# Reordering the first weight loads, thinning the idle matmuls and dropping implied waits in a sliding-window attention and expert-layer kernel

## The chip, the cores and the metric

One core of one Trainium2 chip runs the whole program. The metric is device microseconds (us) per execution; lower is better. In the text S is one moment: the start of the first matmul of the second expert projection. The views name the engines PE (TensorE), DVE (VectorE), ACT (ScalarE), POOL (GpSimd) and SP (SyncE). A load or a transpose by DMA lands when its last part has arrived, and its time runs from issue to landing. TensorE's array has a slow state at the start: in the kernel before, the starts of matmuls of 128 columns are 107 ns apart until about 5.05 us, and 55 to 56 ns after it.

## The reference

Attention over 8 batches, 8 heads, 576 positions and head size 64, where each query sees only keys at most 32 positions away; then an expert layer on 4,608 tokens: 512 to 2,048, squared ReLU, back to 512.

```python
scores = scale * np.matmul(q, k.transpose(0, 1, 3, 2))
mask = np.abs(pos[:, None] - pos[None, :]) <= 32
scores = np.where(mask, scores, -1000000000.0)
attn = softmax(scores)                          # max, exp, sum, divide
x = np.matmul(attn, v).transpose(0, 2, 1, 3).reshape(4608, 512)
h = x @ w_in                                    # first projection
r = np.maximum(h, 0.0)
out = (r * r) @ w_out                           # second projection
```

## The kernel before

The kernel does not state its instruction order. It records operations with their reads and writes, and a list scheduler with assumed durations searches for one order for each engine; then it fills pauses of TensorE with idle matmuls and adds the semaphore waits. So every constant below can move instructions far away from the place where it seems to act.

```python
WARM, COLD, DENSE, SPARSE, EXTRA = 36000, 6000, 1.15, 0.95, 6     # idle matmuls
SIZES = (3,) * 9 + (4,) * 9                # chunks of a score group, after batch 0
ORDER = ("k01 q01 v00 v01 v02 k03 q03 v03 k04 q04 w10 v04 w11 w12 w13 k05 q05 ..."   # start of the loads
# ... (cut)
    def fill(self, out):
        at = 1200
        for op in sorted((o for o in out if o.eng == "PE"), key=lambda o: o.start):
            gap = min(op.start, WARM, self.first.start) - at
            one = 107 if at < COLD else 54
            for k in range(int((gap - 60) * (DENSE if at < COLD else SPARSE) // one) + (EXTRA if op is self.first else 0)):
                # ... (cut: one idle matmul of 128 columns on zeros)
# ... (cut), in emit: a wait is left out only if this engine already waited for as much of this semaphore
            for s, v in need.items():
                if waited.get((op.eng, s), 0) >= v:
                    continue
                waited[(op.eng, s)] = v
                e.wait_ge(sems[s] if s in sems else dsems[s], v)
# ... (cut), in vd_half: odd V products need V shifted by 64 rows, copied on VectorE
            self.p.rec("DVE", lambda e, d=dst, c=src: e.tensor_copy(d, c), reads=rd,
                       writes=[("vd", b % 2, s, lo) for s in range(s0, s1)], key=key, dur=80 + 145 * (s1 - s0), att=True)
# ... (cut), in xturn3: x of a trip of three chunks, transposed by DMA; plan is an allowance in ns
                self.p.rec("SP", lambda e, w=w, np=np, t0=t0: e.dma_start(
                    self.XT[:, :, t0:t0 + np], self.XR[0:np, 2 * y + w, :], transpose=True), ...)
                self.p.ops[-1].plan = 1500
```

In the names of the loads, w10 to w13 are the quarters of the first projection's weights; v03 and v04 are the V pieces that this text calls four and five, and k04 is the one that the texts call the fourth K piece. A chunk is 64 queries of one batch, nine to a batch. An odd chunk goes from its V piece through the copy `vd`, the product (line 778 before, 794 after), the division `xr` on VectorE, and a transpose on TensorE (807 before, 823 after) to `xt`, which the first projection reads (826 before, 842 after). The expert layer works in tiles of 512 tokens; tile 0 does 16 first-projection groups of 16 matmuls of 128 columns. "The third group" below is the third of these.

The softmax here doesn't subtract the row's maximum and nothing guards it: scores larger than these inputs give would overflow.

## Time and profile before

| what | before | how to read it |
|---|---|---|
| device time, first measurement | 300.18 us (299.93 to 300.94) | median of 3 runs |
| span of the profiled execution | 298.4 us | some 1.8 us of the device time lie outside it |
| TensorE busy | 98% | the bound; the rest is in the prediction |
| first group, fourth group | 18.21, 22.13 us | starts, in the order of time |
| S | 35.75 us | TensorE is full from here on |
| waits of TensorE after S | 0.43 us | one, ahead of tile 3 |
| idle matmuls | 103 of 128 columns | they compute nothing |

The kernel before in the order of time on TensorE (start, duration, engine, line, operation, output and inputs, tile, count), from the second group to S. After 22.13 no pause of any length is left:

```profile
19.57 1.06 PE L826 MATMUL ht<-xt,w 128*128 128x128 bf16 x16
...
20.73 1.05 PE L826 MATMUL ht<-xt,w 128*128 128x128 bf16 x16
21.89 0.40 PE L807 MATMUL outp<-identw,xr 128*128 128x128 bf16 x4
22.13 2.06 PE L826 MATMUL ht<-xt,w 128*128 128x128 bf16 x34
...
35.75 1.89 PE L919 MATMUL outp<-w,gt 128*128 128x512 bf16 x8
```

### The profile page before, as it was taken

To read this page: it belongs to the slowest core of one execution; us is meant where nothing else is said; L and a number is where in the kernel's file an instruction comes from. 1 tells how busy PE (TensorE), PEld (TensorE's weight loads), DVE (VectorE), ACT (ScalarE), POOL (GpSimd) and SP (SyncE) were. 2 spreads that over 40 slices of the span, in tenths; PEclk is the share of its full clock that TensorE was granted. 3 is DMA by queue.
4 is the path that set the end of the run, shared out by engine and by line. 5 is a ranking of instruction groups with operands and counts; after the bars stand their busy time and mean duration, and the time that the engine had idled before them with its cause. 6 is when DMAs were issued, how large, how long until landed. Compare 5 with 4: busy or idle time off the path is not lost.

```text
span 298.4 us, 7058 instructions
## 1 busy us (share of the span) xinstructions
PE 293.1 (98%) x2789; PEld 172.0 (58%) x2789; DVE 175.7 (59%) x428; ACT 160.5 (54%) x261; POOL 105.2 (35%) x131
## 2 busy tenths in 40 slices
PE   7899999999999999999999999999999999999996
PEld 7799855867668754544444545544445544444445
DVE  5864755674979966866386666773827682322200
ACT  3466543656657654763555656636645565444411
POOL 8999841332425434351254353313520000000000
PEclk9999999999999999999999999999999999999999
DMA  9999999999999999999499999999992230000022
GB/s 153 166 202 170 206 174 194 174 162 165 187 176 131 133 156 149 159 131 187 63 138 153 173 139 171 117 140 148 126 174 81 64 82 9 35 35 35 36 88 90
DMA packets 166817, 39.34 MB, mean 132 GB/s; under 512 B 157824, under 2 KB 162304, under 8 KB 166784
## 3 DMA queue, kind: packets, MB, share of 16 engines
q0 software_dynamic: 113120, 17.90, 89.8%
q1 hardware_dynamic: 46512, 11.15, 25.2%
q10 hardware_dynamic: 7152, 9.83, 10.1%
q8 instruction: 22, 0.36, 0.5%
q14 instruction: 11, 0.09, 0.1%
HBM read 36.70 MB, written 9.44 MB: 155 GB/s over the span
## 4 chain that ended last, share of the span: by engine, by line
PE 95%; DMA 2%; DVE 2%; issue 0%; POOL 0%; POOLq 0%
PE outp L919 41%; PE ht L867 28%; PE ht L849 7%; PE ht L826 7%; PE sc L703 3%; PE sc L647 3%; DMA qraw<-in_q_dram 2%; PE sc L495 1%; DVE vd L547 1%; PE outp L416 1%; PE sc L895 1%; PE outp L895 1%; DVE xr L791 1%; PE ht L495 0%; PE sc L751 0%; PE outp L807 0%
## 5 line engine op out<-in xcount | busy, mean ns | idle before, releaser
L919 PE MATMUL outp<-w,gt 128*128 128x512 bf16 x560 | 134.5, 379 | 0.0
L882 DVE TENSOR_TENSOR gt<-rt 128x512 bf16<-128x512 bf16 x144 | 59.5, 420 | 62.2 <-ACT rt L873 53.6
L867 PE MATMUL ht<-xt,w 128*128 128x512 bf16 x384 | 93.7, 379 | 0.3 <-issue 0.3
L919 PEld LDWEIGHTS outp<-w,gt 128*128 128x128 bf16 x560 | 52.9, 98 | 58.9
L873 ACT ACTIVATE rt<-ht 128x512 bf16<-128x512 f32 x96 | 57.4, 598 | 51.4 <-PE ht L867 48.9
L867 PEld LDWEIGHTS ht<-xt,w 128*128 128x128 bf16 x384 | 36.3, 98 | 41.9 <-issue 0.4
L469 POOL DMA_DIRECT2D qraw<-in_q_dram x39 | 33.6, 863 | 57.4 <-PE ht L867 20.6
L469 POOL DMA_DIRECT2D kraw<-in_k_dram x39 | 33.6, 860 | 35.1 <-PE ht L867 17.2
L535 POOL DMA_DIRECT2D vx<-in_v_dram x40 | 34.6, 866 | 21.3 <-PE ht L867 13.3
L684 DVE TENSOR_TENSOR pt<-e,mask 128x512 bf16<-128x512 bf16 (+1 forms) x63 | 29.9, 508 | 19.9 <-ACT e L668 19.1
L926 ACT ACTIVATE oe<-outp 128x512 f32<-128x512 f32 x35 | 20.9, 597 | 35.0 <-PE outp L919 34.9
L668 ACT ACTIVATE e<-sc 128x1024 bf16<-128x1024 f32 (+1 forms) x36 | 31.8, 917 | 6.4 <-PE sc L647 6.3
L727 DVE TENSOR_TENSOR xr<-pf,rs 128x512 bf16<-128x512 f32 (+1 forms) x42 | 27.5, 682 | 0.4
L826 PE MATMUL ht<-xt,w 128*128 128x128 bf16 x384 | 23.8, 219 | 0.0
L849 PE MATMUL ht<-xt,w 128*128 128x256 bf16 x192 | 23.3, 273 | 0.0
L826 PEld LDWEIGHTS ht<-xt,w 128*128 128x128 bf16 x384 | 21.7, 98 | 0.3
L720 DVE COPY pf<-sc 128x520 f32<-128x520 f32 x21 | 14.6, 697 | 8.8 <-PE sc L703 8.6
L849 PEld LDWEIGHTS ht<-xt,w 128*128 128x128 bf16 x192 | 18.0, 98 | 3.1
L717 ACT ACTIVATE pf<-sc 128x520 f32<-128x520 f32 x21 | 12.6, 602 | 13.0 <-PE sc L703 11.4
L834 ACT ACTIVATE rt<-ht 128x512 bf16<-128x512 f32 x24 | 14.2, 599 | 9.1 <-PE ht L826 8.8
L855 ACT ACTIVATE rt<-ht 128x512 bf16<-128x512 f32 x24 | 14.3, 600 | 6.0 <-PE ht L849 4.3
L722 DVE TENSOR_TENSOR pf<-pf 64x520 f32<-64x520 f32 x21 | 14.6, 697 | 2.2 <-ACT pf L717 1.2
(83 smaller groups left out, 180.3 us busy)
## 6 DMA issues: line engine op xcount, KB each, us to landing
out_dram<-oe ACTq DMA_DIRECT2D x35, 256.0 KB, 2.9
kraw<-in_k_dram POOLq DMA_DIRECT2D x30, 128.0 KB, 5.7
qraw<-in_q_dram POOLq DMA_DIRECT2D x30, 128.0 KB, 5.9
vx<-in_v_dram POOLq DMA_DIRECT2D x24, 128.0 KB, 5.4
w<-in_moe_w_in_dram POOLq DMA_DIRECT2D x4, 512.0 KB, 10.2
w<-in_moe_w_out_dram POOLq DMA_DIRECT2D x4, 512.0 KB, 16.4
vx<-in_v_dram POOLq DMA_DIRECT2D x16, 96.0 KB, 5.3
xt<-xr SPq DMA_TRANSPOSE x36, 4.0
```

The lines of the kernel that those rows point to most:

```text
L469: self.p.rec("POOL", lambda e: e.dma_start(dst, src), writes=[("fraw", b, t, x)], old=[("fraw", b - 2, t, y + (b == 2))], reads=self.pace( ...
L535: self.p.rec("POOL", lambda e: e.dma_start(self.VX[b % 2][r:r + n, s, :, 0:64], self.v[b, :, t0:t0 + n, :].rearrange("h p d -> p h d")), w ...
L668: self.p.rec("ACT", lambda e, d=dst, a=src: e.activation(d, a, ACTF.Exp, scale=0.125), reads=["s" + x for x in ("AC", "BD")[h]], writes=[( ...
L684: self.p.rec("DVE", lambda e: e.tensor_tensor(pt, ee, mb, ALU.mult), reads=[("e", g // 2)] + rd, writes=[("ptt", k)], old=old, key=key + k ...
L727: self.p.rec("DVE", lambda e, w=w, np=np: e.tensor_tensor(bass.AP(self.XR, 512 * (2 * y + w), [[2048, np], [64, 2], [128, 4], [1, 64]]), b ...
L826: mm = e.matmul(ht[:, 128 * (d % 4):128 * (d % 4) + 128], self.W1[:, ft, 128 * d:128 * d + 128], self.XT[:, ft, t0:t0 + 128], start=(ft == ...
L849: mm = e.matmul(ht[:, 256 * (d % 2):256 * (d % 2) + 256], self.W1[:, ft, 128 * d:128 * d + 128], self.XT[:, ft, 64 * s0:64 * s0 + 256], st ...
L867: mm = e.matmul(ht[:], self.W1[:, ft, 128 * d:128 * d + 128], self.XT[:, ft, 512 * T:512 * T + 512], start=(ft == 0), stop=(ft == 3))
L873: self.p.rec("ACT", lambda e: e.activation(rt[:], ht[:], ACTF.Relu), reads=[("ht", k % 2)], writes=[("rt", k % 4)], key=key, dur=560)
L882: self.p.rec("DVE", lambda e: e.tensor_tensor(g, r, r, ALU.mult), reads=[("rt", k % 4)], writes=tags, key=key, dur=430)
L919: mm = e.matmul(op, gt[:, d, 128 * u:128 * u + 128], self.W2[:, d, :], start=(d == 0), stop=(d == 15))
L926: self.p.rec("ACT", lambda e: e.activation(oe[:], op, ACTF.Copy), reads=[tag], writes=[("oe", x % 4)], key=key, dur=560)
```

## The change

Its intent: begin the expert layer sooner (the first weight quarter ahead of two V pieces), do not let idle matmuls delay real ones, take a load of copying off VectorE at the start, do more small score groups early and large ones late, and leave out waits that another wait already implies. Its core:

```diff
-WARM, COLD, DENSE, SPARSE, EXTRA = 36000, 6000, 1.15, 0.95, 6
+FIRST, WARM, COLD, DENSE, SPARSE, LASTF = 4000, 36000, 6000, 1.15, 0.7, 0.4
-SIZES = (3,) * 9 + (4,) * 9
+SIZES = (3,) * 13 + (4,) * 6
+VDACT = ((0, 0), (2, 0))
-ORDER = ("k01 q01 v00 v01 v02 k03 q03 v03 k04 q04 w10 v04 w11 w12 w13 ...
+ORDER = ("k01 q01 v00 v01 v02 k03 q03 k04 q04 w10 v03 w11 v04 w12 w13 ...
@@ fill @@
-        at = 1200
+        at = FIRST
@@ (cut: idle matmuls of 192 to 512 columns, fewer ahead of the first group) @@
@@ emit @@
-            for s, v in need.items():
-                if waited.get((op.eng, s), 0) >= v:
+            seen = known[op.eng]
+            while need:
+                s = max(need, key=...)              # the one that implies most of the others first
+                v = need.pop(s)
+                if seen.get(s, 0) >= v:
                     continue
-                waited[(op.eng, s)] = v
                 e.wait_ge(sems[s] if s in sems else dsems[s], v)
+                for x, y in at[(s, v)].items():     # what was known where that count was reached
+                    seen[x] = max(seen.get(x, 0), y)
@@ vd_half @@
+            if not b and (s0, lo) in VDACT:
+                self.p.rec("ACT", lambda e, d=dst, c=src: e.activation(d, c, ACTF.Copy), ...)
@@ load_w1 @@
-                   ... move=(32, 82 if d else 95, 500))
+                   ... move=(32, 82, 500 if d > 1 else 1300))
@@ (cut: memsets at the start merged) @@
```

In the built kernels the idle matmuls go from 103 with 13,184 columns to 15 with 6,848, the score groups after batch 0 from 18 to 19, and the waits over all engines from 1,525 to 1,169.

More of the change, by code (lines that the diff above doesn't have):

```diff
@@ L35 @@
 DEPTH, POST, BACK = 4000, {"POOL": 1500, "SP": 1000, "ACT": 1000}, {"POOL": 2500, "SP": 4000, "ACT": 4000}
-ORDER = ("k01 q01 v00 v01 v02 k03 q03 v03 k04 q04 w10 v04 w11 w12 w13 k05 q05 k10 q10 v10 k11 q11 v11 "
+ORDER = ("k01 q01 v00 v01 v02 k03 q03 k04 q04 w10 v03 w11 v04 w12 w13 k05 q05 k10 q10 v10 k11 q11 v11 "
          "w20 w21 w22 w23 k12 q12 v12 k13 q13 v13 k14 q14 v14").split()
@@ L315, in fill @@
             one = 107 if at < COLD else 54
-            for k in range(int((gap - 60) * (DENSE if at < COLD else SPARSE) // one) + (EXTRA if op is self.first else 0)):
+            cols = max(0, int((gap - 60) * (DENSE if at < COLD else LASTF if op is self.first else SPARSE) / one * 4)) * 32
+            t = at
+            while cols >= 192:
                 w = Op()
-                w.eng, w.fn, w.dma, w.deps, w.i = "PE", self.idle, None, {self.idle_on}, op.i
-                w.inc, w.val, w.sem, w.start, w.end, w.dur, w.key = False, None, None, min(at + one * k, op.start - 1), 0, one, -99
+                n = min(cols, 512)
+                w.eng, w.fn, w.dma, w.deps, w.i = "PE", (lambda e, n=n: self.idle(e, n)), None, {self.idle_on}, op.i
+                w.inc, w.val, w.sem, w.start, w.end, w.dur, w.key = False, None, None, min(t, op.start - 1), 0, one * n // 128, -99
                 out.append(w)
+                t, cols = t + w.dur, cols - n
             at = max(at, op.start + op.dur)
@@ L336, in emit @@
                 total[op.dma] = dcount[op.dma[0]] = dcount.get(op.dma[0], 0) + 16
-        waited = {}
+        known = {e: {} for e in engs}
+        at = {}
         for op in self.ops:
@@ L344, in emit @@
                 need[d.sem] = max(need.get(d.sem, 0), d.val)
-            for s, v in need.items():
-                if waited.get((op.eng, s), 0) >= v:
+            seen = known[op.eng]
+            while need:
+                s = max(need, key=lambda s: (s in sems, sum(v <= at.get((s, need[s]), {}).get(x, 0) for x, v in need.items() if x != s)))
+                v = need.pop(s)
+                if seen.get(s, 0) >= v:
                     continue
-                waited[(op.eng, s)] = v
                 e.wait_ge(sems[s] if s in sems else dsems[s], v)
+                for x, y in at[(s, v)].items():
+                    seen[x] = max(seen.get(x, 0), y)
             ins = op.fn(e)
@@ L355, in emit @@
                 op.sem, op.val = s, total[op.dma]
+                info = at.setdefault((s, op.val), {s: op.val})
+                for x, y in seen.items():
+                    info[x] = max(info.get(x, 0), y)
                 ins.then_inc(dsems[s], 16)
@@ L359, in emit @@
                 op.sem, op.val = op.eng, count[op.eng]
+                at[(op.sem, op.val)] = {**seen, op.eng: op.val}
                 ins.then_inc(sems[op.eng], 1)
@@ L415, in setup_idle @@
         self.p.idle_on = self.p.ops[-1]
-        self.p.idle = lambda e: e.matmul(self.OUTP[1][:, 0:128], self.ZZ[:, 0:128], self.ZZ[:, 0:128], start=True, stop=True)
+        self.p.idle = lambda e, n: e.matmul(self.OUTP[1][:, 0:n], self.ZZ[:, 0:128], bass.AP(self.ZZ, 0, [[128, 128], [0, n // 32], [1, 32]]),
+                                            start=True, stop=True)
     def setup_masks(self, key):
@@ L437, in setup_rest, with setup_ptz @@
     def setup_rest(self, i, key):
+        self.ms("DVE", [("vxone", i)], self.VX[i][:, :, :, 64:VS], 1.0, key, 130)
         for s, r in ((0, 0), (4, 96)):
-            self.ms("DVE", [("vxz", i, s)], self.VX[i][r:r + 32, s, :, :], 0.0, key, 160)
-        self.ms("DVE", [("vxone", i, 0)], self.VX[i][32:64, 0, :, 64:VS], 1.0, key, 80)
-        self.ms("DVE", [("vxone", i, 1)], self.VX[i][64:128, 0, :, 64:VS], 1.0, key, 80)
-        self.ms("DVE", [("vxone", i, 2)], self.VX[i][0:96, 4, :, 64:VS], 1.0, key, 80)
-        self.ms("DVE", [("vxone", i, 3)], self.VX[i][:, 1:4, :, 64:VS], 1.0, key, 120)
-        self.ms("DVE", [("ktpad", i, 0)], self.KT[i][:, :, 0:32], 0.0, key)
-        self.ms("DVE", [("ktpad", i, 1)], self.KT[i][:, :, 32 + S_:KW], 0.0, key)
-    def setup_ptz(self, i, key):
-        for j in range(4):
-            self.ms("DVE", [("ptz", i)], self.PT[:, 768 * i + 192 * j + 64:768 * i + 192 * j + 128], 0.0, key, 70)
+            self.p.rec("DVE", lambda e, s=s, r=r: e.memset(self.VX[i][r:r + 32, s, :, :], 0.0), reads=[("vxone", i)],
+                       writes=[("vxz", i, s)], key=key, dur=160)
+        self.ms("DVE", [("ktpad", i)], bass.AP(self.KT[i], 0, [[4 * KW, 128], [KW, 4], [32 + S_, 2], [1, 32]]), 0.0, key, 160)
+    def setup_ptz(self, key):
+        self.ms("DVE", ["ptz"], bass.AP(self.PT, 64, [[2304, 128], [192, 12], [1, 64]]), 0.0, key, 300)
     def pieces(self, b):
@@ L545, in vd_half @@
             src = vx[64 - 64 * lo:128 - 64 * lo, s0 + lo:s1 + lo, :, :].rearrange("p s h d -> p (s h d)")
-            rd = list(tie) + [("vxl", b % 2, s + lo) + u for s in range(s0, s1) for u in ((), (1,))] + [("vxone", b % 2, k) for k in range(4)]
-            self.p.rec("DVE", lambda e, d=dst, c=src: e.tensor_copy(d, c), reads=rd,
-                       writes=[("vd", b % 2, s, lo) for s in range(s0, s1)], key=key, dur=80 + 145 * (s1 - s0), att=True)
+            rd = list(tie) + [("vxl", b % 2, s + lo) + u for s in range(s0, s1) for u in ((), (1,))] + [("vxone", b % 2)]
+            to = [("vd", b % 2, s, lo) for s in range(s0, s1)]
+            if not b and (s0, lo) in VDACT:
+                self.p.rec("ACT", lambda e, d=dst, c=src: e.activation(d, c, ACTF.Copy), reads=rd, writes=to, key=key,
+                           dur=200 + 560 * (s1 - s0), att=True)
+            else:
+                self.p.rec("DVE", lambda e, d=dst, c=src: e.tensor_copy(d, c), reads=rd, writes=to, key=key,
+                           dur=80 + 145 * (s1 - s0) if b else 120 + 300 * (s1 - s0), att=True)
     def load_w1(self, d, key):
@@ L552, in load_w1 @@
         self.p.rec("POOL", lambda e: e.dma_start(self.W1[:, :, 512 * d:512 * d + 512], src),
-                   writes=[("w1", d)], dma=(f"w1{d}", 0), key=key, dur=770, move=(32, 82 if d else 95, 500))
+                   writes=[("w1", d)], dma=(f"w1{d}", 0), key=key, dur=770, move=(32, 82, 500 if d > 1 else 1300))
     def load_w2(self, d, key):
@@ L562, in qk_tags @@
         i = b % 2
-        rd = [("ktpad", i, 0), ("ktpad", i, 1)]
+        rd = [("ktpad", i)]
         for x, (t0, n) in enumerate(self.pieces(b)):
@@ L690, in v_tags @@
             return [("vd", i, s, 0), ("vd", i, s, 1)]
-        return [("vxl", i, s), ("vxl", i, s, 1)] + [("vxone", i, k) for k in range(4)] + ([("vxz", i, s)] if s in (0, 4) else [])
+        return [("vxl", i, s), ("vxl", i, s, 1)] + [("vxone", i)] + ([("vxz", i, s)] if s in (0, 4) else [])
     def av3(self, n, w):
@@ L780, in f @@
             return mm
-        self.p.rec("PE", f, reads=self.v_tags(b, c) + [("pt", x), ("ptz", x)], writes=[tag], key=key, dur=240, att=True)
+        self.p.rec("PE", f, reads=self.v_tags(b, c) + [("pt", x), "ptz"], writes=[tag], key=key, dur=240, att=True)
     def evac(self, n, m, gi, k):
@@ L977, in build @@
         self.setup_rest(0, K + 3)
-        self.setup_ptz(0, K + 2)
-        self.setup_ptz(1, K + 2)
-        self.setup_ptz(2, K + 2)
+        self.setup_ptz(K + 2)
         self.setup_rest(1, -20)
```

## The prediction

> **What bounds the kernel now.** I read the busy shares and the chain first, then the order of time on TensorE, then the landings of the loads.
>
> ```profile
> PE 293.1 (98%) x2789; PEld 172.0 (58%) x2789; DVE 175.7 (59%) x428; ACT 160.5 (54%) x261; POOL 105.2 (35%) x131
> ...
> PE 95%; DMA 2%; DVE 2%; issue 0%; POOL 0%; POOLq 0%
> ```
>
> TensorE is busy 98% of 298.4 us and makes up 95% of the chain; no other engine is over 59%. The 300.18 us on the device are that span and some 1.8 us outside it. A busy matrix engine is not always a useful one, so I looked for work that computes nothing, in the order of time:
>
> ```profile
> 2.77 2.13 PE L416 MATMUL outp<-zz 128*128 128x128 bf16 x18
> ...
> 5.64 0.78 PE L416 MATMUL outp<-zz 128*128 128x128 bf16 x11
> ...
> 17.32 1.05 PE L416 MATMUL outp<-zz 128*128 128x128 bf16 x16
> 18.21 1.06 PE L826 MATMUL ht<-xt,w 128*128 128x128 bf16 x16
> ```
>
> Line 416 is the idle matmul on zeros. 18 of them in 2.13 us are 107 ns apart by their starts, 11 in 0.78 us are 55 ns apart: the array leaves its slow state at about 5.05 us (the spacing changes inside the group of transposes at 4.7 us). The last 16, 0.89 us from start to start, stand directly ahead of the first matmul of the expert layer. When could that one have begun? Its weight quarter:
>
> ```profile
> L552 POOL DMA_DIRECT2D w<-in_moe_w_in_dram x1: 832/832/832, 9.7 to 9.7; - x1
> DMA to landing us min/median/max: 7.8/7.8/7.8
> ```
>
> Issued at 9.66, landed 7.8 later, at 17.5. So 0.7 us of the 18.21 are idle matmuls that ran over the landing. The same view gives the second, third and fourth quarter 20.6, 23.1 and 25.7, V piece five (10.41 + 7.7) 18.1: the loads land in the order of issue, a quarter every 2.55 us, a V or K piece of 128 tokens every 0.84 us. The load stream has no gaps from 7 to 41 us.
>
> After 18.21 I compared the spacing of successive matmul starts with what their columns need (216 ns for 512, 56 for 128). Only two waits remain in 280 us: 0.27 us at 21.6 (a transpose waits for xr) and this one:
>
> ```profile
> 111.21 0.41 PE L703 MATMUL sc<-vx,pt 128*128 128x65 bf16 x8
> 111.88 0.59 PE L867 MATMUL ht<-xt,w 128*128 128x512 bf16 x2 [0.27 <-issue]
> ```
>
> The last P·V matmul starts at 111.42, the next at 111.88: about 0.43 us lost. It is the first one of tile 3; the transpose by DMA of its last tokens was issued at 105.15 and took 6.6 us to land, 111.8. Then each score group (line 647) costs about 0.10 us on entry and 0.105 on exit beyond its columns, where 64-row matmuls meet 128-row ones. The end is thus the start of the saturated stretch, plus fixed work, plus these.
>
> [...] 107 against 55 ns, and 4.06 us from the first matmul (0.99) to the change. [...] The trace shows 22 packets of 16384 bytes, the first at 11.90, the next at 19.15 and 26.00. From the piece that lands next on, the last of 16 engines trails the first by 1.3 us; earlier by 0.4.
>
> **The change, part by part.**
>
> *Load order.* Ahead of the first quarter one V piece less: 17.48 - 0.84 = 16.64. Piece four lands where the quarter did, 17.48; second quarter one piece of 96 tokens earlier (0.62): 20.0; piece five about 20.6; quarters three and four unchanged. The changed program has the first expert group before the fifth odd V product and only one idle matmul (512 columns, 0.21 us) ahead of it.
>
> *Idle matmuls.* 103 of 128 columns become 15 of 192 to 512, 6,848 columns instead of 13,184. Those until 4 us go, so the slow state probably lasts until 7.5 to 9 us instead of 5.05. Then the eight fp32 transposes at 7.91, 0.93 us fast, cost up to 0.9 us more. 88 fewer pairs put the first instruction refill (before: around the 144th matmul) at about 15.7 us.
>
> *Two V copies to ScalarE.* DVE runs without pause from 8.6 to 15.7 us, seven V copies of 0.3 to 0.7 us in it. It sheds two, 0.54 and some 0.3 us, just where the slow array adds up to 0.9; I let them cancel. ScalarE has gaps there (0.6, 1.5 and 0.5 us).
>
> *The start, walked.* With durations of the rows before: fourth K piece 13.3, scores of chunks 4 and 5 at 13.55 (before 14.38), exp until 15.0, masks behind xr 15.7 to 16.45, product of chunk 4 at 16.35, idle matmul until 16.85, first expert group 16.85 (before 18.21). Then the gain shrinks. Chunk 5 wants V piece four: 17.48, copy 0.4, so 18.0 instead of 17.75. Group two 18.28 to 19.17. The transpose behind it waits for xr, which DVE takes after a reciprocal and a mask: about 20.0. Group three about 20.55, product of chunk 7, group four about 21.7. Before, group four starts at 22.13 with one transpose (0.22) more behind it. Gain 22.13 - 21.7 - 0.2 = 0.2 us. If the later refill lets the quarter and piece four land 1 us earlier, the gain is up to 0.9. I take 0.4.
>
> *Later fours.* 9 threes and 9 fours become 13 and 6: 18 groups become 19, +0.2 us. The same 504 score matmuls.
>
> *Implied waits out.* 1,525 waits become 1,169 over the engines. The few single ones that the trace shows take about 20 ns; all except TensorE's (436 to 334) are on engines with slack, and TensorE's spacing shows no cost. 0 us.
>
> *New schedule.* In column time the product that completes tile 3 moves from 9.8 to 10.9 us ahead of its first matmul. It needed about 10.3 before; the 0.43 us should go, three chances in four: -0.35. Tile 4 has 9.1 us instead of 10.5, with 8 needed in emptier stretches (134.7 to 142.3 for its group); tile 2's first half 12.2 instead of 13.1 where 11.5 was needed. I set +0.1 for new bubbles.
>
> Sum: -0.4 + 0.2 - 0.35 + 0.1 = -0.45 us; 300.18 - 0.45 = 299.7.
>
> **Rivals.** (1) *The slow array decides.* If it stays slow well past 9 us[...], every early step stretches, and the first expert group starts after 18 us: 300.5 to 301.5. [...] Against it: from 4.1 to 6.9 the transposes and 1,440 idle columns are dense[...]. (2) *The loads give the gain back.* V pieces four and five come later, and the second projection's last quarter lands at 41.3 with its use at 42.0: slack 0.7 us, so a larger start gain could be cut there. That leaves 300.0 to 300.3. (3) *The start pays in full.* First group at 16.85 and no waits behind it: 1.1 us net, with tile 3's bubble gone 298.8. Against it: the xr chain above.
>
> **Range and chances.** Everything that can move is in the first 22 us or in two bubbles of under half a microsecond; 2% is 6 us, a third of the whole start-up. Faster by 2% would need a start-up of 12 us, which the second quarter's landing at 20 forbids. Slower by 2% would need a wait in every tile, or a long slow array. The runs of before alone spread from 299.93 to 300.94. Range 298.8 to 300.8.
>
> **What would show it.** Right: first expert group at 16.6 to 17.2 with one idle matmul before it; its quarter landed by 16.7; the array's spacing halved only after 7 us; V piece four near 17.5 and a pause of TensorE before chunk 5's product or the next transpose; fourth expert group at 21.0 to 21.9; no gap before tile 3; 19 score groups. Wrong: first group after 17.6, expert matmuls 107 ns apart, or pauses of TensorE after 25 us that sum to over 0.5 us.

In the trace of before, its page lists queue q8, kind "instruction", with 22 packets and 0.36 MB; the prediction calls the first of them the first instruction refill. It came at 11.90 us, behind the 144th weight load; that 88 pairs fewer would put it at 15.7 us is my estimate from that place. The 7.5 to 9 us for the slow state are an estimate too: the 4.06 us from the first matmul to the change, counted from the 4 us at which the idle matmuls now begin, give 8.1.

## The result

A ratio here is the mean time of one kernel's fast runs over the mean of the other's of the same rounds, so it is not quite the ratio of the medians quoted.

| | before | after |
|---|---|---|
| median | 300.06 us (299.76 to 300.94, 4 runs) | 300.44 us (300.26 to 300.68, 4 runs) |
| ratio | | 1.0008, 95% interval 0.9985 to 1.0031 |
| span of the profiled execution | 298.4 us | 298.7 us |

The time is the same within 2%. The predicted 299.7 us is 0.7 us under the median, which lies inside the predicted range. First the page of the kernel after:

```profile
PE 288.4 (97%) x2665; PEld 166.3 (56%) x2701; DVE 174.3 (58%) x407; ACT 161.1 (54%) x265; POOL 105.5 (35%) x131
...
PE 87%; DMA 5%; POOL 3%; DVE 2%; issue 1%; ACT 0%; POOLq 0%; DVEq 0%
```

Two traps are in it. The 4.7 us less of busy TensorE are not a gain: they are idle matmuls that are gone, and 36 matmuls whose records are missing from this trace (2,701 weight loads against 2,665 matmuls). A missing record of a 512-column matmul looks like a pause of 0.22 us (the starts of two such matmuls are 216 ns apart), so pauses of just that length are not counted below. And the chain's share of TensorE fell from 95% to 87% because the chain now runs through loads; the bound has not changed.

The kernel after on TensorE, in the order of time. The bracket is the idle time before a group and what released it:

```profile
7.99 1.09 PE L506 MATMUL ht<-oe,pf 128*128 128x128 f32 x8
...
16.74 1.07 PE L842 MATMUL ht<-xt,w 128*128 128x128 bf16 x16 [0.62 <-DMA w<-in_moe_w_in_dram]
18.28 0.20 PE L794 MATMUL sc<-vd,pt 128*128 128x65 bf16 x1 [0.48 <-DVE vd L563]
...
18.54 1.05 PE L842 MATMUL ht<-xt,w 128*128 128x128 bf16 x16
20.32 0.40 PE L823 MATMUL outp<-identw,xr 128*128 128x128 bf16 x4 [0.72 <-DVE xr L807]
...
20.80 1.05 PE L842 MATMUL ht<-xt,w 128*128 128x128 bf16 x16
...
21.93 1.95 PE L842 MATMUL ht<-xt,w 128*128 128x128 bf16 x32
```

The first group starts 1.47 us earlier than before (16.74 against 18.21), the second 1.03, the third does not start earlier at all (20.80 against 20.73), and the fourth is 0.20 earlier with one transpose of 0.22 us still behind it. So nothing of the 1.47 us is left. Two pauses took it: 0.48 ahead of a product that needs the V copy, and 0.72 ahead of the transpose that needs `xr`. The same stretch on VectorE:

```profile
17.41 0.81 DVE L563 COPY vd<-vx 64x528 bf16<-64x528 bf16 x1 [1.98 <-DMA vx<-in_v_dram]
18.26 0.43 DVE L643 TENSOR_TENSOR pt<-e,mask 128x512 bf16<-128x512 bf16 x1
18.71 0.38 DVE L563 COPY vd<-vx 64x528 bf16<-64x528 bf16 x1
19.02 0.18 DVE L805 RECIPROCAL rs<-sc 128x8 f32<-128x8 f32 x1
19.24 0.42 DVE L643 TENSOR_TENSOR pt<-e,mask 128x512 bf16<-128x512 bf16 x1
19.58 0.68 DVE L807 TENSOR_TENSOR xr<-sc,rs 128x512 bf16<-128x512 f32 x1
```

VectorE stood idle for 1.98 us, until V piece four landed at 17.39, and then had six operations in a row in front of the transpose, 2.85 us from 17.41 to 20.26. The load that was moved back became the start of the chain.

The first of the six deserves a second look. The same copy of 64 x 528 takes 0.29 us elsewhere, 0.81 here and 0.38 at 18.71. GpSimd, in the same stretch, is issuing loads for the next batch:

```profile
17.08 1.03 POOL L480 DMA_DIRECT2D kraw<-in_k_dram  x1
17.95 1.02 POOL L480 DMA_DIRECT2D qraw<-in_q_dram  x1
18.82 1.03 POOL L546 DMA_DIRECT2D vx<-in_v_dram  x1
```

Each issue runs until the next begins (the recorded durations overlap a little). The long copy ends at 18.22, which is 0.27 us after the issue at 17.95 begins; the one of 0.38 ends at 19.09, 0.27 after the one at 18.82. My reading, an estimate from these durations, is a copy of 0.29 us that does not proceed before the issue it meets is almost over. What the traces show is the place of the ends: over the fourteen profiled executions, 94 of these copies lie in the first 25 us; 31 take 0.31 us or less, and all 63 longer ones, up to 0.85 us, have the start of a GpSimd issue inside them and end 0.10 to 0.31 us after it. (Issues follow each other so closely that most of the short copies meet such a start too; it is the place of the end that tells.) Not every part of an issue goes with a long copy: all ten copies that begin within the first 0.22 us of an issue take 0.29 us, while the issue's record runs on. The mask multiplications beside them (line 643) stay at 0.41 to 0.43. No view shows by what an issue would hold a copy up.

The second half of the result is late. Before, tile 3 waited 0.43 us for its x. That wait is absent after the change (its first matmul follows without a bracket), but the first half of tile 2 waits now. SyncE before, then SyncE after and TensorE after, at tile 3:

```profile
105.15 1.26 SPq L738 DMA_TRANSPOSE xt<-xr  x1
```

```profile
104.58 1.27 SPq L539 DMA_TRANSPOSE qt<-qraw  x1
105.89 1.29 SPq L754 DMA_TRANSPOSE xt<-xr  x1
```

```profile
112.23 1.03 PE L883 MATMUL ht<-xt,w 128*128 128x512 bf16 x4
```

The new order gave this transpose no more room. From its issue to the moment at which its user was due there are 6.3 us before (105.15 to 111.45) and 6.3 after (105.89 to 112.23): `xr` was ready at 105.10, but SyncE was still issuing the transpose of a Q piece. What differs is the transfer, 6.6 us before and 5.9 after. e1 below, with the order of before, drew 5.9 us and did not wait either; e6, with the late order of after, drew 6.5 us (landed at 111.84, first matmul at 111.89) and waited about 0.2 us. So the absence of this wait is not shown to be the work of the change.

TensorE after at tile 2:

```profile
85.99 1.92 PE L865 MATMUL ht<-xt,w 128*128 128x256 bf16 x16 [0.40 <-DMA xt<-xr]
```

The bracket says 0.40, since the end of a matmul is modelled. By the starts, the next matmul was due at 85.43 and came at 85.99: 0.56 us. What it waited for is the transpose of x by DMA. Before and after, the issues near 78 us and their landings:

```profile
L738 SPq DMA_TRANSPOSE xt<-xr x1: 1190/1190/1190, 78.0 to 78.0; - x1
...
DMA to landing us min/median/max: 6.4/6.4/6.4
```

```profile
L754 SPq DMA_TRANSPOSE xt<-xr x1: 1189/1189/1189, 78.0 to 78.0; - x1
...
DMA to landing us min/median/max: 8.0/8.0/8.0
```

Both are issued within 0.1 us of each other; one takes 6.4 us, the other 8.0, and its user came 0.9 us earlier in the new order (the 256-column matmuls of this half begin at 86.33 before). Slack and a slow transfer met.

**A sum that closes.** Since TensorE is full after S, each span can be taken apart: S, plus 259.7 us of fixed work, plus 0.22 us for the nineteenth score group where there is one, plus the waits after S, plus 2.5 us after the last matmul starts. 259.7 and 2.5 are read from the kernel before; the others must then close without a free term, and they do, within about 0.1 us. (The first record of the second projection is missing in the trace of after; S is inferred as 35.74 from the next one, and a later execution of the same kernel, below, has it at 35.74.)

| execution | S | groups | waits after S | sum | span |
|---|---|---|---|---|---|
| before | 35.75 | 0 | 0.43 (tile 3) | 298.4 | 298.4 |
| after | 35.74 | 0.22 | 0.56 (tile 2) | 298.7 | 298.7 |
| after, second execution (e9) | 35.74 | 0.22 | 0.20 (a score group at 161) | 298.4 | 298.3 |

### The profile page after: what moved, and what is told of

Read it like the earlier page. It is cut to its first block, busy times and chain, and to the rows that moved or that the text cites. A ratio compares the mean times of both kernels' runs of the same rounds, so it can differ in the third digit from the quotient of the medians.

```text
span 298.7 us, 6569 instructions
## 1 busy us (share of the span) xinstructions
PE 288.4 (97%) x2665; PEld 166.3 (56%) x2701; DVE 174.3 (58%) x407; ACT 161.1 (54%) x265; POOL 105.5 (35%) x131
## 4 chain that ended last, share of the span: by engine, by line
PE 87%; DMA 5%; POOL 3%; DVE 2%; issue 1%; ACT 0%; POOLq 0%; DVEq 0%
PE outp L935 38%; PE ht L883 28%; PE ht L842 7%; PE ht L865 6%; PE sc L719 3%; DMA xt<-xr 3%; PE sc L663 3%; DMA vx<-in_v_dram 3%; POOL kraw L480 1%; POOL vx L546 1%; POOL qraw L480 1%; PE sc L506 1%; PE sc L911 1%; PE outp L911 1%; DVE vd L563 1%
## 5 line engine op out<-in xcount | busy, mean ns | idle before, releaser
L935 PE MATMUL outp<-w,gt 128*128 128x512 bf16 x535 | 132.0, 379 | 1.6 <-issue 0.5
L480 POOL DMA_DIRECT2D qraw<-in_q_dram x39 | 34.3, 881 | 51.6 <-PE ht L883 28.2
L480 POOL DMA_DIRECT2D kraw<-in_k_dram x39 | 34.4, 881 | 38.9 <-PE ht L883 18.7
L546 POOL DMA_DIRECT2D vx<-in_v_dram x40 | 35.7, 894 | 23.3 <-PE ht L883 10.7
L842 PEld LDWEIGHTS ht<-xt,w 128*128 128x128 bf16 x384 | 21.7, 98 | 1.2 <-DMA w<-in_moe_w_in_dram 0.9
```

What stands on the lines that cost most here:

```text
L480: self.p.rec("POOL", lambda e: e.dma_start(dst, src), writes=[("fraw", b, t, x)], old=[("fraw", b - 2, t, y + (b == 2))], reads=self.pace( ...
L546: self.p.rec("POOL", lambda e: e.dma_start(self.VX[b % 2][r:r + n, s, :, 0:64], self.v[b, :, t0:t0 + n, :].rearrange("h p d -> p h d")), w ...
L842: mm = e.matmul(ht[:, 128 * (d % 4):128 * (d % 4) + 128], self.W1[:, ft, 128 * d:128 * d + 128], self.XT[:, ft, t0:t0 + 128], start=(ft == ...
L935: mm = e.matmul(op, gt[:, d, 128 * u:128 * u + 128], self.W2[:, d, :], start=(d == 0), stop=(d == 15))
```

## The experiments

My theory after the result: (A) the start gains nothing because V piece four, moved behind the first weight quarter, and its chain on VectorE set the third group; (B) the late part is one wait for x in the place of another, which of them occurs being partly chance. Rivals: (C) the long slow state of the array, with few early idle matmuls, eats the start; (D) one single part costs time and the others pay for it. All twelve runs gave correct results. The rounds were run in three calls, the second on another chip than the other two; the kernel before had a median of 300.28 us in the first (11 runs, one slow one of 305.14 left out of the ratios), 300.31 in the second and 299.97 in the third.

### Parts alone on the kernel before

**e1_waits**: only the new `emit`.

```diff
-        waited = {}
+        known = {e: {} for e in engs}
+        at = {}
 (and the loop as in the change)
```

> The kernel before with only the implied waits out; the same instructions in the same order on every engine. Theory (waits cost nothing, TensorE is full and the other engines have slack): span within 0.2 us of 298.4, ratio 0.999 to 1.001, first expert group at 18.2. Rival (the removed waits on TensorE, 436 to 334, are on the path at about 20 ns each): 2 us less, ratio 0.993.

Measured: 300.07 us (299.7 to 300.22), ratio 0.999 (0.9978 to 1.0003). In the profiled execution S is 36.12 and no wait follows it; the span is 298.3. It shows how far two executions of one order can differ: the second weight quarter landed at 21.25 instead of 20.60, S came 0.37 us later, and tile 3 did not wait. Leaving out the implied waits is worth nothing that 6 runs can show.

**e2_idle**: only the constants and `fill` with fewer, wider idle matmuls (16 of them here).

```diff
-WARM, COLD, DENSE, SPARSE, EXTRA = 36000, 6000, 1.15, 0.95, 6
+FIRST, WARM, COLD, DENSE, SPARSE, LASTF = 4000, 36000, 6000, 1.15, 0.7, 0.4
```

> The kernel before with only the fewer idle matmuls (16 instead of 103). Theory (the idle matmuls only hid behind loads; the third expert group waits for the second weight quarter at 20.6): first group at 17.5 to 17.7 instead of 18.21, third at 20.6 to 20.8 as before, span -0.15 to +0.1 us. Refill theory: the first 16 KB instruction packet moves from 11.9 to about 14 or 15 us, and the spread between the first and last engine of the fourth-K-piece load, which lands before it, falls from 1.4 to about 0.6 us. Rival (the idle matmuls ahead of the first group cost their 0.7 us): span -0.7 us, 297.7.

Measured: 301.07 us (300.06 to 301.69), ratio 1.0023 (1.0005 to 1.004): a small loss, its interval excludes 1. Its profiled execution has S at 35.96 and loses most at tile 3:

```profile
112.90 0.82 PE L872 MATMUL ht<-xt,w 128*128 128x512 bf16 x3 [1.10 <-DMA xt<-xr]
```

By starts this is 1.27 us, against 0.43 before. The transpose was issued at 105.46 and landed at 112.86, 7.4 us later, against 6.6 before. The start itself is 0.2 us worse: the slow state lasted until 9.48 here, and the products of chunk 4 came at 17.07 instead of 16.37, so that the removed idle matmuls freed nothing and the first group came at 18.23.

The refill theory held for the fourth K piece in this one profile. The first packet of queue q8 came at 15.19 here, and that piece ended 0.38 us later on its last engine than on its first; before, with the packet at 11.90, it was 1.42 us. The kernel after agrees: 0.63 us for the same piece, ahead of the packet at 14.45, and 1.63 us for the first weight quarter, behind it.

**e3_order**: only the order of the loads and the line in `load_w1`.

```diff
-ORDER = ("k01 q01 v00 v01 v02 k03 q03 v03 k04 q04 w10 v04 w11 w12 w13 ...
+ORDER = ("k01 q01 v00 v01 v02 k03 q03 k04 q04 w10 v03 w11 v04 w12 w13 ...
```

> The kernel before with only the load order. Theory (V piece four becomes the limit): first quarter lands near 16.7, V piece four near 17.4, TensorE pauses ahead of the product of chunk 5 or the transpose behind it, and the fourth expert group starts no more than 0.3 us earlier than 22.13; the product of tile 2 stands 12.2 us of column time ahead of its use as in the changed kernel (13.1 before), so a wait of 0.3 to 0.6 us for the transposed x shows at tile 2's first group, and none at tile 3. Span -0.2 to +0.4. Rival (the earlier quarter pays): fourth group by 21.3, span 297.6 or less.

Measured: 300.28 us (300.13 to 300.86), ratio 1.0004 (0.999 to 1.0018). The quarter landed at 16.62, but the first group started only at 18.46, behind products and 12 idle matmuls that are put there whatever lands. Then the V chain. TensorE, and in a second view VectorE:

```profile
21.27 0.40 PE L807 MATMUL outp<-identw,xr 128*128 128x128 bf16 x4 [0.62 <-DVE xr L791]
```

```profile
17.40 1.70 DVE L547 COPY vd<-vx 64x528 bf16<-64x528 bf16 x2
```

V piece four landed at 17.32, its two copies took 1.70 us (they end at 18.23 and 19.09, each 0.27 us behind the start of an issue of GpSimd), and the transpose waited for `xr` as in the whole change. S is 36.69, 0.94 later than before. For A: the load order alone makes the start worse, by the same chain. No wait follows S in this execution (the expected one at tile 2 did not come), so the loss shows as 299.0 of span against 298.4. It is one of the two slowest of the six runs (300.84); in the faster ones the start or the waits must have been better, which their times alone do not tell apart.

**e4_sizes**: only the score groups.

```diff
-SIZES = (3,) * 9 + (4,) * 9
+SIZES = (3,) * 13 + (4,) * 6
```

> The kernel before with only 13 threes and 6 fours. Theory: one more score group, +0.2 us on TensorE; tile 2 has 13.3 us (13.1), tile 3 10.65 (9.8), so the 0.43 us wait at tile 3 shrinks to 0 to 0.2: span -0.3 to +0.2. Rival (the group sizes are what cost the changed kernel its 0.3 us): +0.3 us or more, with the wait at tile 3 still there.

Measured: 300.99 us (300.61 to 301.85), ratio 1.0028 (1.0009 to 1.0046), the largest loss of a single part. The profiled execution has S at 35.85, the nineteenth group, and again tile 3:

```profile
114.20 0.59 PE L867 MATMUL ht<-xt,w 128*128 128x512 bf16 x2 [0.69 <-DMA xt<-xr]
```

By starts 0.86 us, for a transpose that took 7.2 us. The sum 35.85 + 259.7 + 0.22 + 0.86 + 2.5 = 299.1 closes on the span of 299.2. So 0.22 us of the loss is the group, as predicted, and in this execution 0.43 more is the longer wait at tile 3; its transpose drew 7.2 us, which is not shown to come from the group sizes. The expectation that this wait would shrink to 0.2 us or less failed.

**e8_vdact**: only the two V copies on ScalarE, with their assumed durations.

```diff
+VDACT = ((0, 0), (2, 0))
+            if not b and (s0, lo) in VDACT:
+                self.p.rec("ACT", lambda e, d=dst, c=src: e.activation(d, c, ACTF.Copy), ...)
```

> The kernel before with only the two V copies on ScalarE (and the true durations of the others told to the scheduler). Theory: DVE's early chain gets shorter by about 0.8 us, so the products of chunks 4 and 5 come 0.5 us or more ahead of 16.37; but the first quarter still lands at 17.5 and the second at 20.6, so the third expert group starts at 20.6 to 20.8 and the fourth gains what the 0.27 us wait for xr was: fourth group at 21.8 to 22.1; span -0.3 to 0. Rival (DVE's chain sets the start): span -0.6 or less.

Measured: 300.16 us (299.54 to 301.07), ratio 1.0001 (0.9985 to 1.0016). The first group comes 0.37 us earlier, at 17.84, and the third waits for its weights:

```profile
21.20 1.07 PE L832 MATMUL ht<-xt,w 128*128 128x128 bf16 x16 [0.71 <-DMA w<-in_moe_w_in_dram]
```

The second quarter landed at 21.15 in this execution. S is 36.05: again an early gain that a load takes back. It had landed at 20.60 before, with the same order of issue, so this delay belongs to the execution as far as the record tells.

D is not settled. The two parts that lose when alone, e2 and e4, did so in their profiled executions mainly at tile 3, through transposes of 7.4 and 7.2 us; whether they drew them by chance in the other runs too is not known. In the new order the group sizes cost nothing that shows: e12 below, with those of the change, is faster than e11 with those of before.

### What sets the start of the changed kernel

**e6_v4first**: the kernel after, with V piece four ahead of the first quarter again and the second quarter directly behind the first.

```diff
-ORDER = ("k01 q01 v00 v01 v02 k03 q03 k04 q04 w10 v03 w11 v04 w12 w13 ...
+ORDER = ("k01 q01 v00 v01 v02 k03 q03 v03 k04 q04 w10 w11 v04 w12 w13 ...
```

> The changed kernel with V piece four put back ahead of the fourth K piece, and the second weight quarter ahead of V piece five: first quarter at 17.5 as before, second at 20.0, V piece five at 20.6. Theory (V piece four at 17.4 is what eats the earlier quarter): the first group starts later than the changed kernel's 16.74, at 17.5 to 17.7, yet no pause follows it before the third group at 20.0; fourth at 21.3 to 21.6 (changed 21.93), start gain 0.3 to 0.6 us. The wait at tile 2 stays or grows by that (same late order), so span 298.0 to 298.7. Rival (the first quarter's landing is the limit): fourth group at 22.6 or later, span 299.3.

Measured: 300.04 us (299.49 to 301.3), ratio 0.9999 (0.9982 to 1.0016). TensorE:

```profile
17.44 1.07 PE L842 MATMUL ht<-xt,w 128*128 128x128 bf16 x16 [0.62 <-DMA w<-in_moe_w_in_dram]
...
20.05 1.05 PE L842 MATMUL ht<-xt,w 128*128 128x128 bf16 x16 [0.18 <-DMA w<-in_moe_w_in_dram]
21.18 1.95 PE L842 MATMUL ht<-xt,w 128*128 128x128 bf16 x32
```

The first group is 0.70 us later than in the change and the fourth 0.75 us earlier: the pauses for the V copy and for `xr` are gone, as A says, and the second weight quarter is the limit instead. S is 0.40 us earlier; 0.45 us of the gain are lost at 25.8, mostly to a Q piece (the bracket there shows 0.29). After S there were 0.33 us at tile 2 and two smaller waits, one of them at tile 3, 0.6 in all, and 35.34 + 262.42 + 0.6 = 298.4 is the span. The time does not show the gain.

**e9_after_again**: the kernel after, unaltered, for a second execution.

```diff
(no edit)
```

> The changed kernel once more, unaltered, for its spread and for a second execution to read. If the array's slow state now lasts a chance length (the profiles so far with few idle matmuls show it left at about 8, 9.5, 11.8 and 12.5 us; those with many at 5.0 to 6.9), its second execution need not agree with the first in the start: first group between 16.7 and 18.1, fourth between 21.9 and 22.9. Median 300.2 to 300.6.

Measured: 300.25 us (300.11 to 300.92, 5 runs), ratio 1.0002 (0.9984 to 1.002). TensorE:

```profile
20.32 0.40 PE L823 MATMUL outp<-identw,xr 128*128 128x128 bf16 x4 [0.73 <-DVE xr L807]
...
21.93 1.95 PE L842 MATMUL ht<-xt,w 128*128 128x128 bf16 x32
...
35.74 1.03 PE L935 MATMUL outp<-w,gt 128*128 128x512 bf16 x4
```

The first quarter landed at 15.54 here, 1.15 us earlier than in the first execution, and the transpose still starts at 20.32 and the fourth group at 21.93, to the hundredth. So neither this quarter nor the 0.62 us that TensorE waited for it in the first execution mattered. Nor did the moment at which V piece four came. VectorE here:

```profile
17.52 0.70 DVE L563 COPY vd<-vx 64x528 bf16<-64x528 bf16 x1 [1.25 <-DMA vx<-in_v_dram]
```

The copy began 0.11 us later than in the first execution and ended at the same 18.22, behind the same issue of GpSimd (at 17.96 here). Tile 2 did not wait: its x landed at 84.03 instead of 85.94, with the same program. That is the chance in B.

**e10_first1200**: the kernel after with idle matmuls from 1.2 us on (22 in all).

```diff
-FIRST, WARM, COLD, DENSE, SPARSE, LASTF = 4000, 36000, 6000, 1.15, 0.7, 0.4
+FIRST, WARM, COLD, DENSE, SPARSE, LASTF = 1200, 36000, 6000, 1.15, 0.7, 0.4
```

> The changed kernel with the idle matmuls of 1.2 to 4 us put back, as 7 wide ones of up to 512 columns instead of 31 of 128, so that few instructions are added; the rest of the order is the same. Theory (the cut of the early idle matmuls keeps the array slow): the slow state is left at 5 to 7 us, the first instruction refill stays later than 13.5, the first group starts at 16.4 to 16.9, the fourth at 21.4 to 21.9; the wait at tile 2 stays; 0.2 to 0.6 us less than the changed kernel of the same call. Rival (the length of the slow state does not matter, the loads set the start): first group at 16.7, fourth at 21.9, no difference beyond 0.15 us.

Measured: 299.97 us (299.39 to 300.55), ratio 0.9988 (0.997 to 1.0007). The array was fast by 3.83 us. VectorE:

```profile
17.74 0.49 DVE L563 COPY vd<-vx 64x528 bf16<-64x528 bf16 x1 [2.27 <-DMA vx<-in_v_dram]
```

The piece came 0.33 us later than in the first execution, the copy ended at 18.23, the fourth group is at 21.94 and S at 35.75; tile 2 waited 0.35 us, its transpose took 7.8. In this execution a clock that is fast 3 to 4 us sooner moves the start by nothing, so C does not explain the profiled execution of the change. And three executions with three landings end the copy at one time, which points to the end of the issue that the copy meets as what sets the start.

The other runs leave a rest of C open. The mean is 0.42 us below that of e9 in the same rounds, which 5 and 6 runs do not tell from noise, and two of the six spans are 297.6; by the sum above S was then 35.2 at most, 0.5 us earlier than in any profile of this start. e5 below, without early idle matmuls, has two spans of 297.8 (S at most 35.4), so this is not the clock's work alone. I have no profile of such an execution.

### The waits for x, and versions put together

**e5_after_late**: the kernel after, with a larger allowance for the transpose of x, so that the scheduler puts its users later.

```diff
-                self.p.ops[-1].plan = 1500
+                self.p.ops[-1].plan = 3500
```

> The changed kernel, with its scheduler told that a transposed x lands 2 us later than it assumed (3500 for 1500 ns of allowance); it moves the first expert group of each tile back: tile 2 has 13.3 us of column time instead of 12.2, tile 3 12.6 instead of 10.9, the start is the same. Theory (the wait of about 0.4 us at tile 2 is a scheduling slack of under 1 us): no wait for xt at tiles 2 to 8, first expert group still near 16.74 and the fourth near 21.9, span 298.2 to 298.4, that is 0.3 to 0.5 us less than the changed kernel. Rival (the DMA transposes are late because of traffic, and the wait moves with the group): a wait of 0.3 us or more stays, span 298.6 to 298.9.

Measured: 300.15 us (299.58 to 300.95), ratio 0.9997 (0.9983 to 1.0011). No wait for x at all in the profiled execution. But that execution was the slowest of the six (spans of the others 297.8 to 298.5, its own 299.1), with S at 36.62. Its first 9 us on TensorE show why:

```profile
8.20 1.97 PE L506 MATMUL ht<-oe,pf 128*128 128x128 f32 x8
```

The same eight matmuls took 1.09 us in the kernel after. The slow state lasted until 12.46 us. This is C, by chance of the execution, and S came 0.88 us later (36.62 against 35.74). It does not follow from every long slow state: in the first execution of the kernel after it ended by 7.99 us, in e9 at about 10.4, where the same eight matmuls took 1.97 us, and S was 35.74 in both.

**e7_best**: e6 with the score groups of before and the larger allowance.

```diff
-SIZES = (3,) * 13 + (4,) * 6
+SIZES = (3,) * 9 + (4,) * 9
-                self.p.ops[-1].plan = 1500
+                self.p.ops[-1].plan = 3500
```

> V piece four ahead as in the run before, 9 threes and 9 fours as before the change (18 groups), and the 2 us more of allowance for the transposed x. Theory: the three losses add: start -0.3 to -0.6, group -0.2, no waits at tiles 2 and 3 (-0.4): span 297.3 to 297.7, ratio to before 0.996 to 0.998. Rival (each only moves a wait): span 298.2 or more, ratio 0.999 or more.

Measured: 299.80 us (299.49 to 302.3), ratio 0.9999 (0.9974 to 1.0025). Five of the six spans are 297.7 to 298.5, and the profiled one is the sixth, 300.5: the slow state until 11.79 us, S at 36.31, and a score matmul that waited 1.5 us for a transpose of Q by DMA at 105 us.

**e11_best1200**: e7 with the early idle matmuls of e10.

```diff
-FIRST, WARM, COLD, DENSE, SPARSE, LASTF = 4000, 36000, 6000, 1.15, 0.7, 0.4
+FIRST, WARM, COLD, DENSE, SPARSE, LASTF = 1200, 36000, 6000, 1.15, 0.7, 0.4
```

> V piece four ahead, 9 threes and 9 fours, 2 us more allowance for the transposed x (the kernel of the e7 run), and the early idle matmuls back as wide ones. Theory: the array is fast by 7 us; first group 17.4 to 17.6, fourth 21.0 to 21.5, no waits at tiles 2 and 3; span 297.3 to 297.8, ratio to before 0.996 to 0.998. Rival (waits for the transposed q, k and x, which an execution draws by chance, take the gain): ratio 0.999 to 1.001, with a wait of 0.5 us or more somewhere after 80 us.

Measured: 300.62 us (299.81 to 303.24), ratio 1.0018 (0.9982 to 1.0054). A miss as a candidate: S is the best of all, 35.04, and waits of 2.3 us after it take more than that back. (One run of 303.24 has a granted clock of 0.994, like the slow one of before; without it the ratio is 1.0006.) TensorE, and in a second view VectorE:

```profile
87.37 0.75 PE L719 MATMUL sc<-vx,pt 128*128 128x65 bf16 x16 [1.57 <-DVE pt L700]
```

```profile
85.48 0.29 DVE L673 COPY ka<-kt 128x512 bf16<-128x512 bf16 x1 [2.91 <-DMA kt<-kraw]
```

VectorE stood for 2.91 us in front of a copy whose input was still being transposed by DMA; the mask that TensorE needed was behind it in VectorE's order.

**e12_best13**: as e11, with the score groups of the change.

```diff
-SIZES = (3,) * 9 + (4,) * 9
+SIZES = (3,) * 13 + (4,) * 6
```

> The same as the e11 run but with the change's 13 threes and 6 fours. Theory: one more score group, 0.2 us more than the e11 run (ratio larger by 0.0007), the same start. Rival (the later fours are worth something, through shorter waits for q, k and x): 0.2 us or more less than the e11 run.

Measured: 299.82 us (299.76 to 300.88), ratio 0.999 (0.9972 to 1.0008). Five of the six runs lie between 299.76 and 299.87. The profiled execution has S at 35.59, no wait after it, and a span of 298.0; 35.59 + 262.42 = 298.0. S is 0.25 us later than in e6. The copy of V piece five, beside issues of GpSimd from 19.70 to 22.83, took 0.72 us instead of 0.29. VectorE in e6 and then in e12:

```profile
20.58 0.29 DVE L563 COPY vd<-vx 64x528 bf16<-64x528 bf16 x1 [0.98 <-DMA vx<-in_v_dram]
```

```profile
20.75 0.72 DVE L563 COPY vd<-vx 64x528 bf16<-64x528 bf16 x1 [1.02 <-DMA vx<-in_v_dram]
```

The fourth group came at 21.18 in e6 and at 21.78 here, partly made up for later. Its interval includes 1, so it is not shown to beat the kernel before, and it did not run with enough rounds against the kernel after to be called better than that.

## Why the prediction was right or wrong

The range held, for the reason given: what can move is a start-up of 22 us and a few waits under a microsecond. The sum inside did not hold: it forecast a small gain, the first pair of profiles shows a small loss, and a range 2 us wide held both. Its terms against the profiled executions of the two kernels:

| term | predicted | measured |
|---|---|---|
| start | -0.4 | -0.01 |
| nineteenth score group | +0.2 | +0.22 |
| implied waits | 0 | 0 (e1) |
| wait ahead of tile 3 | -0.35 | -0.43 (by luck, see below) |
| new bubbles | +0.1 | +0.56 |
| sum | -0.45 | +0.34 (medians +0.38) |

The terms are those of one pair of executions: S of the order of before was 35.75 and, in e1, 36.12. One of the prediction's own signs of being wrong came true: the pauses after 25 us sum to 0.56, over its 0.5.

**Landings: right where the start rests on them.** First quarter 16.69 (predicted 16.64), V piece four 17.39 (17.48), second quarter 19.91 (20.0), V piece five 20.59 (20.6). First group 16.74 (16.85), one idle matmul ahead of it. The first packet of queue q8 (kind "instruction") came at 14.45, sooner than the predicted 15.7 and behind the 142nd weight load (144th before), and the quarter was not helped: its last engine trailed the first by 1.63 us, against 1.33 before. The fourth K piece landed at 12.29, a microsecond ahead of the predicted 13.3, and the product of chunk 4 came at 15.49 instead of 16.35, which only made TensorE wait longer for the quarter.

**"The start, walked": this step failed.** It had the right chain, the `xr` behind V piece four, and mis-sized its first link, "copy 0.4". The copy took 0.81. The product came at 18.28 instead of 18.0, the transpose at 20.32 instead of about 20.0, the third group at 20.80 instead of 20.55, the fourth at 21.93 instead of 21.7. Its own formula then gives 22.13 - 21.93 - 0.22 = -0.02, no gain at all. Setting 0.4 us, above the 0.2 that the walk itself had given, for the sake of an earlier landing that might help, added to the error: in e9 and e10 neither an earlier quarter, nor a piece that landed 0.11 and 0.33 us later, nor the clock moved this start.

The prediction had seen "seven V copies of 0.3 to 0.7 us" and taken the spread as scatter. It is not scatter: each of the long ones ends 0.10 to 0.31 us behind the start of an issue of GpSimd. With a free copy of 0.29 us and the second one also at 0.29 instead of 0.38, the chain would be some 0.6 us shorter and the fourth group at about 21.3; this is an estimate from the durations above, and no run took the issues away. In e6, with V piece four ahead of the quarter again, the fourth group is 0.75 us earlier, the pauses of the V chain are gone, and the second quarter is the limit.

**Idle matmuls: right in kind, milder in size.** The slow state ended between 7.0 and 7.99 us (predicted 7.5 to 9). The eight fp32 transposes that could have cost 0.9 us more just missed it: 1.09 us, as before. In e5 and e9 they did not miss it: 1.97 us. With idle matmuls from 0.99 us on, the slow state ended at 5.0 to 6.9 us in the profiles up to e8 and by 3.83 in e10; with little work before 4 us it ended by 7.99 us in the first execution of after, at 9.48 in e2, about 10.4 in e9, 11.79 in e7 and 12.46 in e5. How full such a stretch has to be is not shown.

**Score groups and implied waits: right**, 0.22 us and nothing measurable.

**"New schedule": right by luck at tile 3, too small an allowance for new bubbles.** The prediction counted the room at tile 3 from the product that completes it, 9.8 us before and 10.9 after. The gain was lost again in SyncE's queue, behind the transposes of K and Q: from the issue to the due moment there are 6.3 us in both orders. The wait was absent because the transpose took 5.9 us instead of 6.6. For tile 2 it had even counted that the slack of the first half falls from 13.1 to 12.2 us "where 11.5 was needed", and relied on the one landing it knew. The transpose took 8.0 us instead of 6.4. In e9 it took 6.1, and the wait was absent; 0.1 us was a fair mean only if the landing time hardly varies, and it varies by 1.9 us between two executions of one program.

**Rivals.** The first (a long slow state) did not occur in the profiled execution of after; e5 and e7 show executions where it does (until 12.46 and 11.79 us). The second (the loads give the gain back) is what happened, through the moved V piece and not through the second projection's weights that it named. The third (the start pays in full) fell to the `xr` chain that was put up against it.

**What stays open.** Which of the late waits occurs differs between executions of one program (tile 2 waited 0.56 us in the first execution of after and not at all in e9; tile 3 waited 0.43 us before and not at all in e1); I have not shown what makes the same transpose by DMA take 6.1 us once and 8.0 another time, where the median of the 36 of an execution is 4.0 us before and 3.9 after. That GpSimd's issue holds the copy up is read from the coincidence in the traces alone, not from a run that takes the issue away; a copy of piece four on ScalarE, where two such copies took a steady 0.63 us in the kernel after, would be the test. And with one profiled execution for most kernels, the waits of the unprofiled runs are inferred from their times only.

## What to carry to other kernels

When a load is moved ahead of another, walk the chain of the load that was moved back, with the durations that the disputed operation has at its worst in the trace, and stop at the point where both orders do the same work: a first matmul that starts 1.5 us sooner is worth nothing if the third does not. Where one instruction of one shape shows several durations, look for what else ends when the long ones end, before writing a mean into a sum. On a full engine, account for a span as start, fixed work, extra work and waits until it closes; that shows in one line which term a change moved. Count the room of a transfer from its issue, not from the work that makes its data ready: a queue in between can eat the difference. A wait with less slack than the spread of its transfer is a matter of chance, so judge it by several executions and not by the one profiled.
